# Carrying scale factors across partitions by DMA transposes of 16-bit powers of two, in a fused attention and Fourier kernel on one core

## The chip, the core and the metric

The kernel runs on one core of a Trainium2 chip. The core has a matrix engine (TensorE, PE in the profile, with its weight loads as PEld), VectorE (DVE), ScalarE (ACT), GpSimd (POOL) and a queue that issues most of the transfers (SyncE, SP). Each engine works through its own list of instructions in order and waits at an instruction until what it depends on is done; so an instruction that waits holds up all that stand behind it in the same list. The engines share an on-chip memory of 128 partitions; products land in banks of a second memory, PSUM, that ACT and DVE read out. The metric is the device time of one execution, in microseconds (us); lower is better.

## What is computed

Two independent layers are computed on inputs of 2048 x 1024, and their outputs are put side by side. Cut to what matters:

```python
def _A_ref(x, wqkv, wo):            # H = 32 heads of Dh = 32, window W = 256
    qkv = (x @ wqkv).reshape(B, S, 3, H, Dh).transpose(2, 0, 3, 1, 4)
    q, k, v = qkv[0], qkv[1], qkv[2]
    scores = einsum("bhqd,bhkd->bhqk", q, k) * Dh ** -0.5
    mask = (i - j >= 0) & (i - j < W)
    p = softmax(where(mask, scores, -1e9), axis=-1)
    o = einsum("bhqk,bhkd->bhqd", p, v)
    return o.transpose(0, 2, 1, 3).reshape(B, S, D) @ wo

def _B_ref(x, seq_re, seq_im, hid_re, hid_im):
    a = einsum("bsd,ed->bse", x, hid_re)
    b = einsum("bsd,ed->bse", x, hid_im)
    return einsum("ts,bse->bte", seq_re, a) - einsum("ts,bse->bte", seq_im, b)

out = concatenate([A_ref(...), B_ref(...)], axis=-1)
```

All inputs and the output are float32.

## The kernel before

**Number format.** A float32 matrix is multiplied as two float16 parts. Each operand is divided by a power of two, its scale, so that it fits float16; `split` (L124) writes the high part on ACT and the remainder, the low part, on DVE. A product is then three passes over float16 parts (`PASSES`, L48), 12 or 24 matmuls into one PSUM bank.

**Scales.** A scale needs the largest value (or mean size) of a whole block, over all 128 partitions. `top` (L142) or `mean` (L150) leaves one number for each partition; `spread` (L157) joins the pieces to one column, `top_...` in the traces. `scale_of` (L166) brings it across the partitions: PE transposes the column, broadcast to 128x128, against an identity matrix (`ident`) into a PSUM tile `pt_...`; DVE takes the maximum of each row, keeps the exponent bits (an AND with 0x7F800000), clamps and shifts it, and takes the reciprocal. There are four such scales for weights and two for inputs in the head of the kernel, two more for inputs behind it, and then two for `wv`, one for `wo`, two for the hidden matrices (`wd`), eight each for the blocks of B's input (`xp`) and for `wk`, four for `wq`, and 32 for blocks of the sequence matrices (`u`).

**Stages.** First the products for q, k and v (`order`, L390), 24 matmuls each, with the preparation of B's operands beside them by a table of due steps (`at`, L397): step n of that table runs just ahead of product n. Then 48 units (`units`, L742): 16 of kind x, for B's hidden transform, and 32 of kind c, for its sequence transform, each made by `seven` (L1027) as seven products instead of eight, in positions 0 to 6 over three banks in the order a, b, a, c, a, b, a. Position 4 ends in bank a and DVE adds it to the output (`add`, L1034, instruction line L1035), after which position 6 adds further products to the same bank. The last stage is the output projection (`po`), in the same form.

**A unit's preparation.** While unit n-2 runs, `u_top` (L754) sums two loaded blocks on ACT (`junk`), `spread` joins the two, and in the last turn `u_scale` (L765) makes the scale; while unit n-1 runs, `u_step` (L793) splits into `un_a`, `un_b`, `un_c` and a part kept in `reg`.

**Attention** runs as a generator (`attention`, L210), advanced by `tick` (L363) a step at a time between the matmuls of the products and units. One block of 128 queries of two heads makes scores `s` on PE, a masked maximum `mx` on DVE, exponentials on ACT, a float16 pair `hl`, and a DMA transpose of `hl` to `t` (L272). Six blocks later `v_step` multiplies by v. After four blocks `o_step` (L322) divides, transposes the result to `ot` by DMA (L335) and lists a store of `ot` to memory (`store_o`), which is issued at L354 in the next fourth block.

**What sets the order.** The program is written in one sequence and a scheduler places instructions on each engine by its own estimate of durations; `issue_after` pins some to follow another. `fixed` pins PE's matmuls to program order, `behind`, `behind_act`, `marks` and `line` (the last of the pinned loads and of the transposes to `t`) pin others. All transfers named here, transposes included, are issued by SP's one list.

Of the kernel before, what the change touches and what calls it, by code (L numbers as in the profile page):

```python
# [9 lines left out]
F32 = mybir.dt.float32  # L10
F32R = mybir.dt.float32r
F16 = mybir.dt.float16
BF16 = mybir.dt.bfloat16
U8 = mybir.dt.uint8
U32 = mybir.dt.uint32
AF = mybir.ActivationFunctionType
ALU = mybir.AluOpType
# [2 lines left out]
P = 128  # L20
S = 2048
D = 1024
H = 32
# [30 lines left out]
def fused_kernel(ctx: ExitStack, tc: tile.TileContext, xa, wqk, wv, wo, xb, wd, cs, out):  # L54
# [23 lines left out]
    tsum = reg1[:, :7 * 8 * CH].rearrange("p (s h k c) -> p s h k c", s=7, h=2, k=4)  # L78
    spare = reg1[:, 7 * 8 * CH:]

    ident = const.tile([P, P], F32, name="ident")
    make_identity(nc, ident)


    upper = const.tile([P, P], F32, name="upper")
# [8 lines left out]
    pshift = const.tile([P, 1], F32, name="pshift")  # L94
    nc.gpsimd.memset(pshift, PSHIFT)

    nbank, units_on = [0], []

    def bank(name):
        nbank[0] += 1  # L100
        return ps_m.tile([P, CH], F32, tag=f"m{nbank[0] % 3}", name=name)
# [31 lines left out]
        return const.tile([P, 2], F32, name=f"sc_{name}")  # L133

    tops, head = {}, [True]


    behind = []
# [18 lines left out]
    def spread(key, n):  # L157
        t = tops.pop(key)
        if n > 1:
            t1 = small.tile([P, 1], F32, tag="top0", name=f"top1_{key}")  # L160
            vec(nc.vector.tensor_reduce, t1, t, axis=AX.X, op=ALU.max)
        else:
            t1 = t
        tops[key] = t1

    def scale_of(key, v, s, down=2.0 ** -14):  # L166

        if head[0]:
            pt = ps_s.tile([P, CH], F32, tag="s", name=f"pt_{key}")[:, :P]
            with tc.issue_after(fixed[0].ins) if fixed else nullcontext():  # L170
                fixed[:] = [nc.tensor.transpose(pt, tops.pop(key).to_broadcast([P, P]), ident)]
        else:
            pt = (ps_v.tile([P, CH], F32, tag="pv", name=f"pt_{key}") if units_on else bank(f"pt_{key}"))[:, :P]
            nc.tensor.transpose(pt, tops.pop(key).to_broadcast([P, P]), ident)
        vec(nc.vector.tensor_reduce, v, pt, axis=AX.X, op=ALU.max)
        vec(nc.vector.tensor_scalar, v.bitcast(U32), v.bitcast(U32), 0x7F800000, None, op0=ALU.bitwise_and)
        vec(nc.vector.tensor_scalar, v, v, 2.0 ** -100, down, op0=ALU.max, op1=ALU.mult)
        vec(nc.vector.reciprocal, s, v)
# [31 lines left out]
    def attention():  # L210
# [127 lines left out]
        for b in range(nblk + LAG):  # L338
            for j in range(2):
                yield (blocks[b][0], blocks[b][2]) if b < nblk else None  # L340
                if b < nblk and j == 0:
                    s_step(b, 0)
                    s_step(b, 1)
                if j == 1 and b % 2 == 0 and b >= LAG:
                    v_step(b - LAG)
                    g, hp, sc, i = blocks[b - LAG + 1]
                    if i == QB - 1:
                        o_step(g, hp, sc)
                if j == 1 and b % 2 == ZAT and 3 <= b < nblk + 4:
                    for m in (b - 3 - (ZAT == 0), b - 2 - (ZAT == 0)):  # L350
                        if 0 <= m < nblk:
                            z_step(m)
                if j == 1 and store_o and (b >= nblk or blocks[b][3] == 3):
                    nc.sync.dma_start(*store_o.pop(0))  # L354
                if j == 1 and b < nblk and blocks[b][3] == 1 and b + 3 < nblk:
                    g, hp, sc, _ = blocks[b + 3]
                    if (g, sc) in ready:
                        do_load(g, hp, sc)
# [38 lines left out]
    def at(n, f, *args):  # L397
        tasks.setdefault(n, []).append((f, args))
# [151 lines left out]
    for (kd, g), n in use.items():  # L550
        if kd in "qk" and n >= 4:
            at(n - 6, w_load, kd, g)
            at(n - 4, w_top, kd, g)
            at(n - 3, w_finish, kd, g)
    for g in range(NG):
        at(max(use["q", g], use["k", g], 11), scores_scale, g)

# [3 lines left out]
        at(n, x_split, 0, (i,), behind_act)  # L561
    at(7, strict.__setitem__, 0, False)
    at(7, head.__setitem__, 0, False)
    at(4, x_top, 2, (0, 1))
    at(5, x_top, 2, (2, 3))
    at(7, x_finish, 2)
# [4 lines left out]
    at(11, x_known)  # L571
    at(11, wv_load, 0)
    at(14, wv_top, 0)
    at(15, wv_scale, 0)
    for i, n in enumerate((15, 16, 16, 17)):
        at(n, wv_split, 0, (i,))
    at(15, wv_load, 1)
    at(18, wv_top, 1)
    at(19, wv_scale, 1)
    for i, n in enumerate((19, 20, 21, 21)):  # L580
        at(n, wv_split, 1, (i,))
    at(20, wv_known)
    def scan(key, ns):
# [292 lines left out]
    at(len(order) - 3, x_left, 0, "c")  # L876


    with tc.tile_pool(name="pa", bufs=2) as pa:
        def qk_out(kd, g, c, ps, f):  # L880
            y = pa.tile([P, 2, CH], F16, tag="yq", name=f"y{kd}{g}_{c}")
            behind_act[:] = [nc.scalar.activation(y[:, 0], ps, AF.Copy, scale=f)]
            behind[:] = [vec(nc.vector.scalar_tensor_tensor, y[:, 1], ps, f, y[:, 0],
                             op0=ALU.mult, op1=ALU.subtract)]
            a = "qk".index(kd)
            nc.sync.dma_start(qk[g, c, a:a + 2, :, :, a].rearrange("j d h t -> (d h) j t"), y)
            nc.sync.dma_start(qk[g, c, 2 - 2 * a, :, :, a].rearrange("d h t -> (d h) t"), y[:, 0])

        def d_out(g):
            qk_out("q", g, 0, direct.pop(g), f0[:, g:g + 1])  # L890

        w_top("q", 0)
        x_top(0, (0, 1, 2, 3))
        d_mm(0, range(0, 4))
        w_scale("q", 0)
        d_mm(0, range(4, 8))
        w_top("q", 1)
        d_mm(1, range(0, 1))
        x_scale(0)
        d_known(0)  # L900
        d_mm(1, range(1, 3))
        w_scale("q", 1)
        d_known(1)
        d_out(0)
        w_split("q", 0)
        w_top("q", 2)
        d_mm(1, range(3, 8))
        x_top(1, (0, 1))
        d_out(1)
        d_mm(2, range(0, 2))  # L910
        w_scale("q", 2)
        d_known(2)
        x_top(1, (2, 3))
        d_mm(2, range(2, 8))
        w_top("q", 3)
        d_mm(3, range(0, 2))
        x_scale(1)
        x_split(1, (0, 1))
        d_out(2)
        d_mm(3, range(2, 4))  # L920
        w_scale("q", 3)
        d_known(3)
        x_split(1, (2,))
        d_mm(3, range(4, 8))
        x_split(1, (3,))
        w_split("q", 1)
        d_out(3)

        for n, (kd, g, c) in enumerate(order):
            if n < 4:  # L930
                continue
            if n == 22:
                first_cm.__exit__(None, None, None)
                att_cm = tc.tile_pool(name="att", bufs=2, side="right")
                cell["att"] = att_cm.__enter__()
                agen[0] = attention()
                upcoming[0] = next(agen[0])
            for f, args in tasks.pop(n, ()):
                f(*args)
            rate[0] = 2 * early * EARLY.get(n, 0.85) / 24  # L940
            ps = bank(f"p{kd}{g}_{c}")
            if kd == "v":
                t = c
                product(ps, lambda h, d: xin[:, t // 4, h, d, t % 4 * P:t % 4 * P + P],
                        lambda h, d: reg2[:, g, h, d])
                y = pa.tile([P, H // 2, VW], F16, tag="yv", name=f"yv{g}_{t}")
                nc.gpsimd.memset(y[:, :, DH:DH + 1], 1.0)
                nc.gpsimd.memset(y[:, :, 2 * DH + 1:], 0.0)
                f = vf[:, g, t // 4:t // 4 + 1]
                pv = ps.rearrange("p (h d) -> p h d", d=DH)  # L950
                behind_act[:] = [nc.scalar.activation(y[:, :, :DH], pv, AF.Copy, scale=f)]
                behind[:] = [nc.vector.scalar_tensor_tensor(y[:, :, DH + 1:2 * DH + 1], pv, f, y[:, :, :DH],
                                                            op0=ALU.mult, op1=ALU.subtract)]
                nc.sync.dma_start(vs[t, :, g * (H // 2) * VW:(g + 1) * (H // 2) * VW],
                                  y.rearrange("p h w -> p (h w)"))
            else:
                u = wun[kd, g]
                product(ps, lambda h, d: u[:, h, d], lambda h, d: xin[:, c, h, d])
                qk_out(kd, g, c, ps, DOWN if kd == "q" else kf[:, c:c + 1])
            if kd == "v" and g == 0 and c % 4 == 3:  # L960
                ready.add((0, c // 4))
            if kd == "v" and g == 1 and c == NT - 1:
                pass
            if kd == "k" and g > 0:
                ready.add((g, c))
# [116 lines left out]
            hook(pos)  # L1082


    units_on.append(True)
    perm, turns = [(nbank[0] + 1 + k) % 3 for k in range(3)], [0]
    with tc.tile_pool(name="pb", bufs=1) as pb:
        ybufs = [pb.tile([P, 2, CH], F32, name=f"y{k}") for k in range(3)]
        ybufs.append(spare[:, 16 * P:].bitcast(F32).rearrange("p (e c) -> p e c", e=2))
        ny = [0]  # L1090
# [154 lines left out]
```

## Time and profile before

| | |
|---|---|
| Time, median of three runs | 1716.21 us (1709.82 to 1716.93) |
| Profiled execution, its own time | 1715.44 us |
| Its span, first to last instruction | 1713.7 us |
| Granted TensorE clock | 1.00 |
| Chain of work that ended last | PE 84%, DMA 5%, DVE 4%, ACT 4% |
| Transfers | 348.63 MB, mean 203 GB/s |
| Transposes by DMA: `t` and `ot` | 256 and 64 |

The page of the profile gives the busy time of each engine, then the span in 40 slices in which a digit is the busy share in tenths. A group of instructions reads "line, engine, operation, output<-inputs, shapes, count | busy us, mean ns of one | idle time of the engine before them, and who ended it". In the list of waits a row reads "engine, its line, who it waited for: us in total, times, longest". In a timeline a row is "start, duration, engine, line, operation, output<-inputs, shapes, count", with idle time before it in brackets. Of an issued transfer "to landing" is the time until its data are there. The chain's 84% for PE, with nothing else above 5%, says that the end is set by what PE does or waits for.

### The profile page before, as it was taken

Reading aid. Unit: us, or ns where it says so; the run is one execution under the profiler, and the core shown is the slowest. Engines: PE = TensorE matmul, PEld = TensorE weight load, DVE = VectorE, ACT = ScalarE, POOL = GpSimd, SP = SyncE. Lnnn points to the kernel's source line nnn. Section 1 sums busy time; section 2 is a strip of 40 time slices with the busy share of each in tenths; the row PEclk is TensorE's granted clock in tenths of the full one; section 3 lists DMA queues with packets and bytes.
Section 4 is the critical chain, followed back from the end, with each engine's and each line's share of the span. In section 5 each row is a group of like instructions: output and inputs, shape, how many; then the busy total and the mean of one; then the engine's idle time right before and its main releaser. Section 6 shows DMA issues by size and latency. Waiting matters only on the chain.

```text
span 1713.7 us, 30874 instructions
## 1 busy us (share of the span) xinstructions
PE 1694.8 (99%) x10999; PEld 852.4 (50%) x10999; DVE 1302.1 (76%) x2225; ACT 1170.1 (68%) x2035; POOL 575.5 (34%) x874
## 2 busy tenths in 40 slices
PE   9999999999999999999999999999999989999999
PEld 4444555555555544555554555545545545444444
DVE  6847788887987788887688886698876698688442
ACT  4566666676877787887687886688876678563322
POOL 0001222344434441444423565434565424411000
PEclk9999999999999999999999999999999999999999
DMA  9747999999998994887998999987999986875431
GB/s 349 245 137 242 252 291 289 271 262 299 243 245 198 215 226 121 206 196 182 229 244 241 196 182 181 223 196 127 197 169 185 203 203 127 166 193 118 117 98 74
DMA packets 469899, 348.63 MB, mean 203 GB/s; under 512 B 376944, under 2 KB 409968, under 8 KB 468848
## 3 DMA queue, kind: packets, MB, share of 16 engines
q1 hardware_dynamic: 462064, 321.48, 74.7%
q0 software_dynamic: 7680, 25.17, 9.2%
q8 instruction: 86, 1.41, 0.4%
q14 instruction: 69, 0.57, 0.1%
HBM read 166.99 MB, written 106.17 MB: 159 GB/s over the span
## 4 chain that ended last, share of the span: by engine, by line
PE 84%; DMA 5%; DVE 4%; ACT 4%; issue 2%; POOL 1%; SPq 0%; ACTq 0%; DVEq 0%; POOLq 0%
PE p_a L114 23%; PE pv L114 14%; PE p_b L114 11%; PE pk L114 9%; PE pq L114 9%; PE p_c L114 6%; PE po_a L114 5%; PE s L114 3%; PE po_b L114 2%; DMA raw_u<-in_cs_dram 2%; DMA t<-hl 1%; PE far L114 1%; PE po_c L114 1%; ACT reg L833 1%; DVE raw_u L791 1%
## 5 line engine op out<-in xcount | busy, mean ns | idle before, releaser
L266 ACT ACTIVATE s<-s,bias,escs 128x256 f32<-128x256 f32 (+1 forms) x512 | 270.1, 528 | 11.7
L284 POOL TENSOR_SCALAR_AFFINE_SELECT z<-t 128x512 f16<-128x512 f16 x224 | 186.4, 840 | 180.4 <-PE pv L114 137.4
L270 DVE TENSOR_TENSOR hl<-s,hl 128x512 f16<-128x512 f32 (+1 forms) x256 | 169.9, 664 | 61.6 <-ACT hl L269 59.5
L259 ACT ACTIVATE bias<-mx,pshift,escs 128x2 f32<-128x2 f32 x256 | 98.2, 384 | 169.3 <-DVE mx L256 168.8
L114 PEld LDWEIGHTS <-reg 128*128 128x128 f16 x1344 | 129.1, 98 | 141.5
L286 POOL TENSOR_SCALAR_AFFINE_SELECT t<-t 128x512 f16<-128x512 f16 x224 | 183.9, 830 | 11.4
L114 PE MATMUL p_a<-reg,un_c 128*128 128x512 f16 x768 | 181.2, 379 | 1.8 <-ACT y L1033 1.3
L114 PE MATMUL pk<-reg,wu_k 128*128 128x512 f16 x768 | 174.4, 379 | 0.0
L256 DVE TENSOR_REDUCE mx<-s 128x2 f32<-128x512 f32 (+1 forms) x256 | 170.7, 667 | 3.4
L114 PE MATMUL pv<-reg,reg 128*128 128x512 f16 x768 | 172.7, 379 | 0.0
L114 PEld LDWEIGHTS <-un_c 128*128 128x128 f16 x1152 | 110.0, 97 | 124.0 <-issue 4.9
L114 PEld LDWEIGHTS <-un_b 128*128 128x128 f16 x1152 | 110.1, 97 | 123.9 <-issue 7.8
L263 POOL TENSOR_SCALAR mark<-bias 128x1 f32<-128x1 f32 x128 | 52.3, 409 | 355.2 <-ACT bias L259 355.0
L114 PEld LDWEIGHTS <-un_a 128*128 128x128 f16 x1152 | 109.8, 97 | 116.2
L269 ACT ACTIVATE hl<-s 128x512 f16<-128x512 f32 (+1 forms) x256 | 148.8, 581 | 13.6 <-DMA t<-hl 8.3
L114 PE MATMUL pq<-reg,wu_q 128*128 128x512 f16 x672 | 151.3, 379 | 0.8 <-DVE reg L121 0.5
L114 PE MATMUL p_a<-reg,un_b 128*128 128x512 f16 x576 | 136.4, 379 | 4.7 <-DVE y L1035 3.0
L114 PE MATMUL p_b<-reg,un_b 128*128 128x512 f16 x576 | 136.3, 379 | 1.2 <-ACT y L1033 1.0
L114 PE MATMUL p_a<-reg,un_a 128*128 128x512 f16 x576 | 136.6, 379 | 0.0
L114 PE MATMUL p_c<-reg,un_a 128*128 128x512 f16 x576 | 136.5, 379 | 0.0
L254 DVE COPY_PREDICATED s<-upper,far 128x256 f32<-128x256 uint32 x224 | 94.2, 420 | 46.0 <-PE s L114 45.0
L114 PEld LDWEIGHTS <-qk 96*128 96x128 f16 x1056 | 87.9, 97 | 64.1 <-DMA qk<-qk 1.9
(208 smaller groups left out, 3154.1 us busy)
## 6 DMA issues: line engine op xcount, KB each, us to landing
raw_u<-in_cs_dram SPq DMA_DIRECT2D x64, 512.0 KB, 4.9
qk<-qk SPq DMA_DIRECT2D x64, 384.0 KB, 5.1
out_dram<-y POOLq DMA_DIRECT2D x72, 256.0 KB, 6.3
raw_wd<-in_wd_dram SPq DMA_DIRECT2D x24, 512.0 KB, 5.3
vs<-yv SPq DMA_DIRECT2D x32, 264.0 KB, 4.2
vt<-vs SPq DMA_DIRECT2D x64, 132.0 KB, 4.2
raw_wo<-in_wo_dram SPq DMA_DIRECT2D x16, 512.0 KB, 9.2
qk<-yq SPq DMA_DIRECT2D x32, 256.0 KB, 3.1
```

The costliest lines, as they stand in the source:

```text
L114: fixed[:] = [nc.tensor.matmul(*args, **kwargs)]
L254: nc.vector.copy_predicated(s[:, :, P:], upper2, d["far"] if nb == 3 else never2)
L256: nc.vector.tensor_reduce(mx, sv, axis=AX.X, op=ALU.max, negate=True)
L259: nc.scalar.activation(bias, mx, AF.Identity, bias=pshift, scale=es)
L263: marks[:] = [nc.gpsimd.tensor_scalar(mark, bias[:, 0:1], 1.0, None, op0=ALU.mult)]
L266: nc.scalar.activation(sv[:, h], sv[:, h], AF.Exp, bias=bias[:, h:h + 1], scale=es)
L269: nc.scalar.activation(hi, sv, AF.Copy)
L270: behind[:] = [nc.vector.tensor_tensor(lo, sv, hi, op=ALU.subtract)]
L284: nc.gpsimd.affine_select(out=z, in_=pk, compare_op=ALU.is_gt, fill=0.0, base=0, pattern=[[0, 4], [-1, P]], channel_multiplier=1)
L286: nc.gpsimd.affine_select(out=pk, in_=pk, compare_op=ALU.is_ge, fill=0.0, base=0, pattern=[[0, 4], [1, P]], channel_multiplier=-1)
L791: nc.vector.tensor_tensor(o, a, b, op=op)
L833: nc.scalar.activation(hi, src, AF.Copy)
```

## The change

Scales past the head no longer use PE. `spread` writes a 128x128 tile `pb` on DVE: the upper 16 bits of each partition's float32 number, ANDed with 0x7F80 and repeated along the row. These 16 bits are a power of two in the format bfloat16. SP issues a DMA transpose of `pb` to `pc`, and `scale_of` takes the maximum of each row of `pc`, then clamps, shifts and takes the reciprocal as before; the AND on the result is gone. The path is switched on at step 11 of the table, so the two scales of inputs that are made behind the head keep the transpose on PE.

The other edits: the store of `ot` is pinned to follow the last transpose or load in `line`; `ident` moves into a spare region that is free in the head; the output tiles of q, k and v share three buffers where there were two for q and k and two for v; scales and splits of the later `wq` and `wk` and of `wv` come one step later in the table.

```diff
         tops[key] = t1
+        if crossing[0]:
+            pb = crossing[0].tile([P, P], F16, tag="pb", name=f"pb_{key}")
+            nc.vector.tensor_scalar(pb.bitcast(U16), t1.bitcast(U16)[:, 1:2].to_broadcast([P, P]), 0x7F80, None,
+                                    op0=ALU.bitwise_and)
+            pc = crossing[0].tile([P, 1, P], F16, tag="pc", name=f"pc_{key}")
+            nc.sync.dma_start_transpose(pc, pb)
+            crossed[key] = pc.rearrange("p a t -> p (a t)").bitcast(BF16)
...
+        if key in crossed:
+            nc.vector.tensor_reduce(v, crossed.pop(key), axis=AX.X, op=ALU.max)
+            nc.vector.tensor_scalar(v, v, 2.0 ** -100, down, op0=ALU.max, op1=ALU.mult)
+            nc.vector.reciprocal(s, v)
+            return
...
-            pt = (ps_v.tile([P, CH], F32, tag="pv", name=f"pt_{key}") if units_on else bank(f"pt_{key}"))[:, :P]
+            pt = bank(f"pt_{key}")[:, :P]
...
-                    nc.sync.dma_start(*store_o.pop(0))
+                    with tc.issue_after(line[0].ins):
+                        nc.sync.dma_start(*store_o.pop(0))
...
-            at(n - 3, w_finish, kd, g)
+            at(n - 3 if n < 16 else n - 2, w_finish, kd, g)
...
+    at(11, lambda: crossing.__setitem__(0, pa))
...
-    at(15, wv_scale, 0)
-    for i, n in enumerate((15, 16, 16, 17)):
+    at(16, wv_scale, 0)
+    for i, n in enumerate((16, 17, 17, 18)):
...
-    ident = const.tile([P, P], F32, name="ident")
+    ident = spare[:, :2 * P].bitcast(F32)
...
-    with tc.tile_pool(name="pa", bufs=2) as pa:
+    with tc.tile_pool(name="pa", bufs=3) as pa:
...
-            y = pa.tile([P, 2, CH], F16, tag="yq", name=f"y{kd}{g}_{c}")
+            y = pa.tile([P, 2, CH], F16, tag="y", name=f"y{kd}{g}_{c}")
...
-                y = pa.tile([P, H // 2, VW], F16, tag="yv", name=f"yv{g}_{t}")
+                y = pa.tile([P, H // 2, VW], F16, tag="y", name=f"yv{g}_{t}")
...
     with tc.tile_pool(name="pb", bufs=1) as pb:
+        crossing[0] = pb
```

How this moves instructions is seen best in the unit stage. First DVE's list in unit 5, of before, from the joined column `top_u` of unit 7 to the addition after position 4 (`y<-p_5_a`) and the one after position 5 (`y<-p_5_b`); `un_c` and `un_b` are splits for unit 6, `s`, `mx`, `hl` and `o` are attention:

```order
L121 TENSOR_REDUCE top_u_8232<-top_u_8153 128x1
L254 COPY_PREDICATED s_8242<-upper,far 128x2x128
L256 TENSOR_REDUCE mx_8248<-s_8242 128x2
L270 TENSOR_TENSOR hl_8194<-s_8182,hl_8194 128x512
L121 SCALAR_TENSOR_TENSOR un_c<-raw_u_1_7756,sc_u_8072,un_c 128x1024
L1035 SCALAR_TENSOR_TENSOR y_6763<-p_5_a,fu_7878,y_6763 128x512
L254 COPY_PREDICATED s_8290<-upper,far 128x2x128
L121 SCALAR_TENSOR_TENSOR un_b<-raw_u_0_7834,sc_u_8072,un_b 128x1024
```

The same stretch in the changed kernel; `sc_u<-pc_u` is the reduction over the transposed tile:

```order
L123 TENSOR_REDUCE top_u_8259<-top_u_8180 128x1
L170 TENSOR_SCALAR pb_u_8261<-top_u_8259 128x128
L269 COPY_PREDICATED s_8273<-upper,far 128x2x128
L271 TENSOR_REDUCE mx_8279<-s_8273 128x2
L179 TENSOR_REDUCE sc_u_8425<-pc_u_8263 128x1
L180 TENSOR_SCALAR sc_u_8425<-sc_u_8425 128x1
L285 TENSOR_TENSOR hl_8221<-s_8209,hl_8221 128x512
L181 RECIPROCAL sc_u_8425<-sc_u_8425 128x1
L788 TENSOR_SCALAR fu_8429<-fa,sc_u_8425 128x1
L123 SCALAR_TENSOR_TENSOR un_c<-raw_u_1_7781,sc_u_8102,un_c 128x1024
L1052 SCALAR_TENSOR_TENSOR y_6787<-p_5_a,fu_7904,y_6787 128x512
```

The whole scale has moved ahead of `un_c` and of the addition after position 4 (L1035 of before is L1052 now). Before, the reduction `sc_u<-pt_u` stood 16 rows behind `top_u`, past both additions.

Second, SP's list at the same unit, of before, from a transpose to `ot` to the store of that `ot`:

```order
L335 DMA_TRANSPOSE ot_1_3_8120<-ohl_1_3_8117 128x4x128
L272 DMA_TRANSPOSE t_8052<-hl_8049 128x8x128
L354 DMA ots<-ot_1_3_8120 128x512
L272 DMA_TRANSPOSE t_8147<-hl_8144 128x8x128
L272 DMA_TRANSPOSE t_8197<-hl_8194 128x8x128
```

and of the changed kernel:

```order
L350 DMA_TRANSPOSE ot_1_3_8147<-ohl_1_3_8144 128x4x128
L287 DMA_TRANSPOSE t_8082<-hl_8079 128x8x128
L287 DMA_TRANSPOSE t_8174<-hl_8171 128x8x128
L173 DMA_TRANSPOSE pc_u_8263<-pb_u_8261 128x1x128
L287 DMA_TRANSPOSE t_8224<-hl_8221 128x8x128
L769 DMA raw_u_0_8390<-in_cs_dram 128x1024
L769 DMA raw_u_1_8523<-in_cs_dram 128x1024
L287 DMA_TRANSPOSE t_8290<-hl_8287 128x8x128
L370 DMA ots<-ot_1_3_8147 128x512
```

The store stood one transpose behind its `ot` and now stands four transposes to `t`, two loads and the new transpose to `pc` behind it.

More of the change, by code (lines that the diff above doesn't have):

```diff
@@ L14 @@
 U8 = mybir.dt.uint8
+U16 = mybir.dt.uint16
 U32 = mybir.dt.uint32
@@ L95, in fused_kernel @@
     nc.gpsimd.memset(pshift, PSHIFT)
-    nbank, units_on = [0], []
+    nbank = [0]
     def bank(name):
@@ L135, in fused_kernel @@
     tops, head = {}, [True]
+    crossing, crossed = [None], {}
     behind = []
@@ L578, in fused_kernel @@
     at(18, wv_top, 1)
-    at(19, wv_scale, 1)
-    for i, n in enumerate((19, 20, 21, 21)):
+    at(20, wv_scale, 1)
+    for i, n in enumerate((20, 21, 21, 22)):
         at(n, wv_split, 1, (i,))
@@ L1082, in seven @@
             hook(pos)
-    units_on.append(True)
     perm, turns = [(nbank[0] + 1 + k) % 3 for k in range(3)], [0]
     with tc.tile_pool(name="pb", bufs=1) as pb:
+        crossing[0] = pb
         ybufs = [pb.tile([P, 2, CH], F32, name=f"y{k}") for k in range(3)]
```

## The prediction

> **What bounds the kernel now.** I read the page first: engine totals, then the 40 slices.
>
> ```profile
> span 1713.7 us, 30874 instructions
> ...
> PE 1694.8 (99%) x10999; PEld 852.4 (50%) x10999; DVE 1302.1 (76%) x2225; ACT 1170.1 (68%) x2035; POOL 575.5 (34%) x874
> ...
> PE   9999999999999999999999999999999989999999
> ...
> DVE  6847788887987788887688886698876698688442
> ```
>
> TensorE (PE) is full in every slice but one, so only two things can shorten the kernel: fewer PE instructions, or less of the 1713.7 - 1694.8 = 18.9 us in which PE stands still. VectorE (DVE) is second, near eight tenths through the middle. Next the waits of PE alone, then the windows over two stages.
>
> ```profile
> PE p_a L114 <- DVE y L1035: 4.4, 6, 1.7
> PE p_a L114 <- ACT p_c L1067: 2.3, 5, 1.1
> ...
> PE s L114 <- DMA qk<-qk: 1.4, 1, 1.4
> ...
> PE pt_u L174 <- DVE o L318: 0.6, 1, 0.6
> ```
>
> ```profile
> 300.00:400.00 100.00, 100.00 (x697) 51.61 (x696) 86.80 (x156) 69.31 (x124) 39.84 (x77) 1.00 1.02 274
> ...
> 920.00:1050.00 130.00, 127.83 (x925) 66.59 (x924) 109.58 (x197) 101.51 (x187) 74.62 (x99) 1.00 0.97 177
> ```
>
> Columns are the stretch, its length, busy time of PE, PEld, DVE, ACT, POOL, then clock, DMA share and GB/s. Where PE waits at all, it mostly waits for one DVE instruction: the addition at L1035 that empties bank a after position 4 of a seven-product unit, so that position 6 may add onto the bank. In the unit stage (920 to 1050 us) DVE works 84% of the time, and that addition is where its lateness becomes PE's.
>
> **The part removed: 57 transposes.** Seven groups at L174 go; the two of pt_x stay, as do those of the head (L171).
>
> ```profile
> L174 PE MATMUL pt_u<-ident,top_u 128*128 128x128 f32 x32 | 8.8, 274 | 0.6 <-DVE o L318 0.6
> ...
> L174 PE MATMUL pt_wk<-ident,top_wk 128*128 128x128 f32 x8 | 2.2, 273 | 0.0
> L174 PE MATMUL pt_xp<-ident,top_xp 128*128 128x128 f32 x8 | 2.2, 273 | 0.0
> L174 PE MATMUL pt_wq<-ident,top_wq 128*128 128x128 f32 x4 | 1.1, 280 | 0.0
> ...
> L174 PE MATMUL pt_wv<-ident,top_wv 128*128 128x128 f32 x2 | 0.5, 272 | 0.0
> L174 PE MATMUL pt_wd<-ident,top_wd 128*128 128x128 f32 x2 | 0.5, 272 | 0.0
> L174 PE MATMUL pt_wo<-ident,top_wo 128*128 128x128 f32 x1 | 0.3, 302 | 0.0
> ```
>
> 32+8+8+4+2+2+1 = 57. Their 274 ns is a duration in a pipeline, not what PE loses. The timeline of PE around one shows the loss:
>
> ```profile
> 630.63 1.03 PE L114 MATMUL p_a<-reg,un_a 128*128 128x512 f16 x4
> 631.49 0.27 PE L174 MATMUL pt_u<-ident,top_u 128*128 128x128 f32 x1
> 631.60 1.89 PE L114 MATMUL p_a<-reg,un_a 128*128 128x512 f16 x8
> ```
>
> Starts are 0.11 us apart, while four products before it took 0.86 us. So 57 x 0.11 = 6.3 us leave PE; without further effects 1715.4 becomes 1709.1.
>
> **The part added: a wait inside DVE's queue.** A scale now goes DVE (pb), SP queue, DMA transpose, DVE again (the reduction over pc). DVE runs in order. By the order of the changed kernel the reduction stands none to six rows behind pb, and in 29 of the 32 units it stands ahead of the L1035 addition after position 4; before, it stood behind both additions and waited only for PE. What is queued behind the waiting reduction is thus the split un_c, that addition, and the attention's DVE work; PE's position 6 waits for the addition. The unit whose order is shown above, in the trace of before:
>
> ```profile
> 682.24 0.14 DVE L121 TENSOR_REDUCE top_u<-top_u 128x1 f32<-128x2 f32 x1
> ...
> 685.10 1.28 DVE L121 SCALAR_TENSOR_TENSOR un_c<-raw_u,sc_u,un_c 128x1024 f16<-128x1024 f32 x1 [0.92 <-ACT un_c L127]
> 686.30 0.74 DVE L1035 SCALAR_TENSOR_TENSOR y<-p_a,fu,y 128x512 f32<-128x512 f32 x1
> ```
>
> ```profile
> 688.23 1.89 PE L114 MATMUL p_a<-reg,un_b 128*128 128x512 f16 x8
> ```
>
> The addition starts 4.06 us after top_u and ends at 687.04; PE takes up position 6 at 688.23: 1.19 us to spare. I took the same three times in all 32 units; the first and the last:
>
> ```profile
> 622.32 0.14 DVE L121 TENSOR_REDUCE top_u<-top_u 128x1 f32<-128x2 f32 x1
> ...
> 625.11 0.74 DVE L1035 SCALAR_TENSOR_TENSOR y<-p_a,fx,y 128x512 f32<-128x512 f32 x1
> ```
>
> ```profile
> 627.81 1.89 PE L114 MATMUL p_a<-wx,un_c 128*128 128x512 f16 x8
> ```
>
> ```profile
> 1520.81 0.14 DVE L121 TENSOR_REDUCE top_u<-top_u 128x1 f32<-128x2 f32 x1
> ...
> 1523.87 0.74 DVE L1035 SCALAR_TENSOR_TENSOR y<-p_a,fu,y 128x512 f32<-128x512 f32 x1
> ```
>
> ```profile
> 1525.68 2.75 PE L114 MATMUL p_a<-reg,un_b 128*128 128x512 f16 x12
> ```
>
> Means over the 32: the addition starts 4.1 us after top_u, ends at 4.8, PE comes at 5.7. The spare time is 0.9 us, and below 0.7 in 17 units.
>
> Now the new chain, with L the time from the end of pb to the landing of pc. No row shows a 128x128 transpose, nor pb. The nearest DVE rows:
>
> ```profile
> L121 DVE TENSOR_REDUCE sc_u<-pt_u 128x1 f32<-128x128 f32 x32 | 9.0, 282 | 8.2 <-PE pt_u L174 8.2
> ...
> L121 DVE TENSOR_SCALAR sc_u<-sc_u 128x1 uint32<-128x1 uint32 x32 | 4.8, 149 | 0.6
> ```
>
> Both pb and the new reduction lie between 0.15 and 0.28 us; I take 0.15 and 0.25, which leaves DVE's work about as it was (one 0.15 and one 0.28 go). For L, the transposes of four tiles (ot) and of eight (t), each row taken from the answer on its tile or line:
>
> ```profile
> L335 SPq DMA_TRANSPOSE ot<-ohl x64: 1188/1213/2481, 194.3 to 1486.7; - x64
> ...
> DMA to landing us min/median/max: 1.7/3.8/10.4
> ```
>
> ```profile
> DMA to landing us min/median/max: 2.3/4.8/14.8
> ```
>
> SP spends 1.2 us issuing even the smallest. Landing counts from the start of the issue. From eight tiles to four the median falls by 1.0 us, 0.25 a tile; one tile would be 3.8 - 3 x 0.25 = 3.05 us. Half an issue of another transpose ahead of it in SP's queue adds 0.6: L = 3.6 us, an estimate. Its ends are 1.7, the least that four tiles took, and 4.8, the median of eight; the 3.6 is nearer the four-tile median, which carries the same fixed part.
>
> In the 29 units the mean work between top_u and pb is 0.2 us and from the reduction to the addition 1.3 us (durations as in the grouped rows, by the new order). The addition then ends 0.1 + 0.2 + 0.15 + L + 0.25 + 1.3 + 0.74 = 2.7 + L after top_u. Against PE's 5.7 that is free up to L = 3.0, and at 3.6 costs 0.6 us a unit, 29 x 0.6 = 17 us. Unit by unit, where spare time cannot be shared, I get 4 us at L = 2.5, 11 at 3.0, 21 at 3.5, 32 at 4.0 and 58 at 5.0, so about 23. I take 20 us.
>
> **The other edits.** The 25 other crossings make DVE wait too, between 80 and 525 us; the pt_wk rows are the first and last of them:
>
> ```profile
> L174 PE MATMUL pt_wk<-ident,top_wk x8: 272/273/275, 81.7 to 523.9; 128*128 128x128 f32 x8
> ```
>  There PE refills one of three banks only two products later, at least 2 x 24 x 0.215 = 10 us; that covers a wait of 3 us: 0, at worst 5 if DVE, 87% busy at 300 to 400 us, lacks the room. Splits of weights one step later still have two steps of 5 us: 0. The shared y buffers and ident in the spare region touch no wait of PE's: 0. The later store of ot frees SP:
>
> ```profile
> SPq L354 <- DMA ot<-ohl: 134.9, 58, 9.1
> ```
>
> SP's queue stood 134.9 us behind that store, 2.3 each; 57 new issues of 1.2 us take 68 back. PE waits for none of the transfers behind it except 1.4 us once, so I put 0 here, and 2 us of gain as the end. Sum: 1715.4 (the profiled execution; span 1713.7 and 1.7 around it; the median of three runs is 0.8 higher) - 6.3 + 20 = 1729 us.
>
> [...]
>
> **Rivals.**
> - *The wait is hidden.* L is 3.0 or less, or DVE reaches top_u earlier because it has nothing else to do: 0 to 11 us of stall, 1709 to 1720 us. For it: the best four-tile landing, 1.7 us, and the 64 KB loads in the row below. Against: the DMA engines are 97% busy in the window of 920 to 1050 us, and 3.8 is the median.
>
> ```profile
> raw_o<-ots SPq DMA_DIRECT2D x128, 64.0 KB, 2.4
> ```
>
>  [...]
> - *The stalls of before go too.* The later store lets transposes land sooner, DVE is less behind, and the 4.4 us on L1035 shrink: 1715.4 - 6.3 - 4.4 - 2 = 1703, range 1701 to 1707.
> - *SP's queue is the price.* The pc transpose sits behind loads that wait for buffers, L is 4.5 to 5: 45 to 58 us, 1754 to 1767.
>
> **How the numbers follow.** Forecast, 1720 to 1741: 0.45. Hidden: 0.33. Stalls go too: 0.10. SP's queue: 0.12. Half a per cent of 1716.2, 8.6 us, is about what a measurement of this kernel tells from no change: faster is below 1707.6, slower above 1724.8. Slower: 0.12 and 0.38 of the forecast's share, 0.50. Faster: 0.10 and 0.06 for the low edge of the hidden case, 0.16. The rest, 0.34, is the same. The range of 8 in 10 runs from 1704, inside the third case, to 1750, which leaves SP's queue out.
>
> **What would show it.** PE: 57 fewer transposes and busy time about 6 us down. DVE: a wait of sc_u on the DMA of pc, 1 to 3 us each, some 60 us in all. PE: p_a waiting for y at the L1035 addition some 25 times instead of 6, for 15 to 30 us. SP: the wait of the store on ot nearly gone. I am wrong if pc lands within 3 us of pb, if the addition is late without PE noticing, or if PE waits elsewhere, for s or pv.

## The result, and the profile after

| | before | changed |
|---|---|---|
| Time, median | 1714.89 us (six runs, 1709.82 to 1718.91) | 1786.51 us (six runs, 1782.17 to 1791.03) |
| Ratio, 95% interval | | 1.042 (1.0394 to 1.0446) |
| Profiled execution: its own time, span | 1715.44, 1713.7 us | 1782.17, 1780.1 us |
| Granted TensorE clock | 1.00 | 0.991 |

The changed kernel is 4.2% slower. The sign was forecast and the size was not: 1729 us was predicted, and the range ended at 1750. The page of the changed kernel answers to the lines shown before: span, busy time of each engine, slices of PE and DVE, and the chain that ended last.

```profile
span 1780.1 us, 30857 instructions
...
PE 1709.4 (96%) x10942; PEld 848.5 (48%) x10942; DVE 1308.0 (73%) x2225; ACT 1167.6 (66%) x2035; POOL 566.2 (32%) x874
...
PE   9999999999999999999998999999999999999999
...
DVE  6757768887887778887687776688687698577542
...
PE 57%; DVE 17%; DMA 9%; ACT 8%; issue 6%; POOL 2%; SPq 1%; DVEq 0%; POOLq 0%; ACTq 0%
```

Two numbers of the PE row tell where to look. PE stands still for 1780.1 - 1709.4 = 70.7 us, against 18.9 before: 51.8 us more. And it is busy for 14.6 us longer although 57 of its instructions are gone (10999 to 10942). Together that is 66.4 us, the whole difference of the spans. The row of slices hardly shows either, since a slice is 44 us long and "9" covers everything above 90%. The chain does: PE's share fell from 84% to 57%, and DVE and the DMA engines took its place.

Next, the waits of PE in the changed kernel (who waited, for whom, us in total, times, longest), and the three largest waits of DVE on the new transposes. `far` is the attention's PSUM tile for the scores of the oldest keys of the window; `p_c` is bank c, which ACT fills with a copy of bank a after position 0.

```profile
PE p_a L116 <- DVE y L1052: 32.4, 19, 4.4
PE far L116 <- DVE s L269: 13.5, 14, 2.3
PE p_a L116 <- ACT p_c L1084: 9.3, 7, 3.9
PE p_a L116 <- DVE sc_u L180: 3.9, 2, 3.5
PE far L116 <- DVE vwd L180: 1.4, 1, 1.4
```

```profile
DVE sc_u L179 <- DMA pc_u<-pb_u: 72.4, 29, 5.9
...
DVE scw L179 <- DMA pc_wk<-pb_wk: 18.4, 8, 5.5
...
DVE vxp L179 <- DMA pc_xp<-pb_xp: 14.3, 6, 5.6
```

The addition after position 4 (L1052, which was L1035) is the largest, as forecast: 32.4 us against 4.4. None of the four rows below it was in the prediction's sum; of them only the copy `p_c` stood in the waits that it showed, with 2.3 us. Two of the rows name an instruction that ended right beside the one that PE needed. At 1076.37 us (`sc_u`, 3.5 us) PE started 0.06 us after the addition's end, and so it did in the other `sc_u` wait on bank a; at 411.01 us (`vwd`) it started 0.05 us after the end of DVE's masking (L269), for which `far` waits. Counted there, PE waited 36.3 us for the addition and 14.9 for the masking.

Two windows place the loss by stage (length, busy time of PE, granted clock, DMA share, GB/s); in the trace of before the same two stages, from 80 us to the first unit product at 566 and from there to the output projection at 1564.5, took 486.0 and 998.5 us.

```profile
80.00:582.60 502.60, 486.59 (x3188) 0.99 0.91 242
582.60:1631.10 1048.50, 999.37 (x6784) 0.99 0.85 181
```

So the qkv stage lost 16.6 us and the units 50.0.

One unit shows the mechanism at full length. The timeline of DVE and then of PE in the changed kernel (start, duration, instruction, and in brackets the idle time before it and who ended it):

```profile
1041.15 0.23 DVE L170 TENSOR_SCALAR pb_u<-top_u 128x128 uint16<-128x128 uint16 x1
1047.31 0.29 DVE L179 TENSOR_REDUCE sc_u<-pc_u 128x1 f32<-128x128 bf16 x1 [5.93 <-DMA pc_u<-pb_u]
1047.52 1.27 DVE L123 SCALAR_TENSOR_TENSOR un_c<-raw_u,sc_u,un_c 128x1024 f16<-128x1024 f32 x1
...
1049.10 0.74 DVE L1052 SCALAR_TENSOR_TENSOR y<-p_a,fu,y 128x512 f32<-128x512 f32 x1
```

```profile
1049.90 1.04 PE L116 MATMUL p_a<-reg,un_b 128*128 128x512 f16 x4 [4.41 <-DVE y L1052]
...
1051.38 3.28 PE L116 MATMUL p_a<-reg,un_b 128*128 128x512 f16 x8
```

DVE finishes pb and has nothing it may do: the next instruction on its list is the reduction over pc, which can start only 5.93 us later. For 1.2 us of that the transpose stood in SP's list behind a transpose to `t`; it landed 4.7 us after the start of its issue at 1042.55 us. The split un_c and the addition, which need nothing from that DMA, stand behind it. PE waits 4.41 us for the addition. Then the second price appears: the eight products that follow take 3.28 us, where eight take 1.89 elsewhere. A window tells why (columns as above):

```profile
1051.00:1052.00 1.00, 1.00 (x6) 0.50 0.98 344
1052.00:1053.00 1.00, 1.00 (x4) 0.50 2.83 224
1053.00:1054.00 1.00, 1.00 (x4) 0.50 0.05 5
```

PE was granted half its clock for 3.41 us, from 1050.77 us on. This trace has eight such stretches, 30.7 us together; PE was busy in 29.7 us of them, so half of that, 14.9 us, went into doing the same work more slowly. Three theories were put to the test. **Theory 1**: the wait in DVE's list stops PE, and the pauses cost clock on top. **Theory 2**: 57 more transposes on SP's list and the DMA engines slow everything. **Theory 3**: the other edits of the change cost the time.

### The profile page after: what moved, and what is told of

Its sections match the earlier page's. It is cut to its first block, busy times and chain, and to the rows that moved or that the text cites. A ratio compares the mean times of both kernels' runs of the same rounds, so it can differ in the third digit from the quotient of the medians.

```text
span 1780.1 us, 30857 instructions
## 1 busy us (share of the span) xinstructions
PE 1709.4 (96%) x10942; PEld 848.5 (48%) x10942; DVE 1308.0 (73%) x2225; ACT 1167.6 (66%) x2035; POOL 566.2 (32%) x874
## 4 chain that ended last, share of the span: by engine, by line
PE 57%; DVE 17%; DMA 9%; ACT 8%; issue 6%; POOL 2%; SPq 1%; DVEq 0%; POOLq 0%; ACTq 0%
PE p_a L116 17%; PE pv L116 8%; PE p_b L116 7%; PE pq L116 6%; DMA pc_u<-pb_u 5%; PE po_a L116 5%; PE p_c L116 4%; PE pk L116 4%; PE po_b L116 2%; DVE mx L271 2%; PE s L116 2%; ACT s L281 2%; DVE raw_u L808 1%; DVE hl L285 1%; DVE reg L851 1%
## 5 line engine op out<-in xcount | busy, mean ns | idle before, releaser
L116 PE MATMUL p_a<-reg,un_b 128*128 128x512 f16 x576 | 146.3, 399 | 34.9 <-DVE y L1052 27.1
L269 DVE COPY_PREDICATED s<-upper,far 128x256 f32<-128x256 uint32 x224 | 94.4, 421 | 37.8 <-PE s L116 37.1
```

Of the source, the lines that this page charges most:

```text
L116: fixed[:] = [nc.tensor.matmul(*args, **kwargs)]
L269: nc.vector.copy_predicated(s[:, :, P:], upper2, d["far"] if nb == 3 else never2)
```

## The experiments

**Late reductions.** All stays as in the changed kernel, but the reduction over pc is pinned behind the last addition or remainder (`hl`, `y`) that was written ahead of it. By the order of the program it stood one to seven rows behind pb and, in 29 units, ahead of both additions; now it stands behind both in all 32.

```diff
         if key in crossed:
-            nc.vector.tensor_reduce(v, crossed.pop(key), axis=AX.X, op=ALU.max)
+            with tc.issue_after(behind[0].ins) if behind else nullcontext():
+                nc.vector.tensor_reduce(v, crossed.pop(key), axis=AX.X, op=ALU.max)
```

> Changed kernel, with the reduction over pc pinned behind the last addition or remainder that was written ahead of it, so that in all 32 units it stands behind both additions on VectorE's list; DMA transposes and all other edits stay. Theory 1 (VectorE's list stands at the reduction and TensorE then waits for the addition and for the scores, and loses clock): 1704 to 1716 us, TensorE's waits for y under 8 us in all, none for far above 1 us, clock 1.00. Theory 2 (57 more transposes load SP's list and the DMA engines): stays at 1775 to 1790. Theory 3 (the other edits): stays at 1775 to 1790.

Measured: 1722.35 us (1710.69 to 1726.55), 1.0033 of before (1.0008 to 1.0059). With every transpose still there, some 64 us of the 72 are gone, and Theories 2 and 3 fall as main causes. DVE's waits on all tiles pc shrink from 122 us (72.4 + 18.4 + 14.3 in the rows above, and 17.1 in four smaller ones) to 20:

```profile
DVE sc_u L180 <- DMA pc_u<-pb_u: 14.6, 2, 13.8
...
DVE vwd L180 <- DMA pc_wd<-pb_wd: 4.3, 1, 4.3
...
DVE vxp L180 <- DMA pc_xp<-pb_xp: 0.8, 1, 0.8
```

The time missed Theory 1's 1704 to 1716. The waits for the addition came out as expected, 2.8 us; but the clock was 0.996 instead of 1.00, and `far` waited 2.9 us where at most 1 was expected. PE's waits show what cost the time: one long pause.

```profile
PE p_a L116 <- ACT p_c L1085: 12.4, 1, 12.4
PE s L116 <- DMA qk<-qk: 2.9, 1, 2.9
PE far L116 <- DVE vwd L181: 2.9, 1, 2.9
PE p_a L116 <- DVE y L1053: 2.8, 5, 1.0
```

Its cause is read from SP's timeline. The transpose for unit 46 was issued right behind eight loads of `raw_wo`, 512 KB each by their shape (128 x 1024 float32), and landed 15.7 us after its issue, the longest of all:

```profile
1496.23 3.95 SPq L224 DMA_DIRECT2D raw_wo<-in_wo_dram  x8
1500.28 1.15 SPq L173 DMA_TRANSPOSE pc_u<-pb_u  x1
```

**The last two units by TensorE.** To see whether that one transpose explains the miss, the kernel with late reductions was run again with the scales of units 46 and 47 by TensorE.

```diff
                     att_cm.__exit__(None, None, None)
+                    crossing[0], id2[0] = None, upper
+                    make_identity(nc, upper)
...
-            pt = bank(f"pt_{key}")[:, :P]
-            nc.tensor.transpose(pt, tops.pop(key).to_broadcast([P, P]), ident)
+            last = id2[0] is not None
+            pt = (ps_v.tile([P, CH], F32, tag="pv", name=f"pt_{key}") if last else bank(f"pt_{key}"))[:, :P]
+            nc.tensor.transpose(pt, tops.pop(key).to_broadcast([P, P]), id2[0] if last else ident)
```

> The kernel with late reductions once more, but the scales of the last two units go by TensorE again (against an identity tile written over the mask, which nobody needs by then). Theory 1, with the loss of the first run put down to the one transpose that landed 15.7 us after its issue, behind eight loads of raw_wo: the pause of 12.4 us and the half clock behind it go, 1703 to 1709 us, clock 1.00. If the loss came from the transposes in general (Theory 2): 1718 to 1724 as in the first run.

Measured: 1711.77 us (1705.77 to 1713.40), 0.9979 (0.9955 to 1.0004). The pause of 12.4 us is gone, and with it 10.6 us (9 by the two ratios, whose intervals do not overlap), so it was the cause of most of the miss; yet the time stays some 3 us above the range that was given. One pause in the qkv stage is left, of the same kind: `far` waits for DVE, which waited for the transpose of `wd`, and again the products behind it are slow (eight in 3.62 us).

```profile
402.25 0.27 PE L116 MATMUL far<-qk 96*128 96x128 f16 x1 [3.53 <-DVE vwd L181]
...
402.84 3.62 PE L116 MATMUL pk<-reg,wu_k 128*128 128x512 f16 x8
```

**The other edits alone.** Every scale goes by TensorE as before, `ident` stays where it was, and what is left of the change is the pinned store of `ot`, the shared y buffers and the later steps.

```diff
-    at(11, lambda: crossing.__setitem__(0, pa))
...
-        crossing[0] = pb
...
-    ident = spare[:, :2 * P].bitcast(F32)
+    ident = const.tile([P, P], F32, name="ident")
```

> All other edits of the change (store of ot pinned, three shared y buffers, scales and splits one step later), but every scale by TensorE as before, and ident where it was. Theory 1: 1710 to 1718 us, as before. Theory 2: the same, since no transposes are added. Theory 3: 1760 or more.

Measured: 1707.65 us (1705.61 to 1709.93), 0.9969 (0.9957 to 0.9982). Theory 3 has the wrong sign: the other edits gain, and the time lies below the 1710 to 1718 of the other two theories too. The same kernel, measured once more beside a kernel shown below:

> The kernel with the other edits alone, once more on the same chip, for the comparison with the kernel above: 1706 to 1709 us, 0.995 to 0.999 of the kernel before.

Measured: 1710.14 us, 0.9962 (0.9945 to 0.9979). The gain is small but both intervals lie below 1, and of all kernels run this one has the lowest ratio.

**The pinned store alone**, to see which of these edits gains: the kernel before with one edit.

```diff
-                    nc.sync.dma_start(*store_o.pop(0))
+                    with tc.issue_after(line[0].ins):
+                        nc.sync.dma_start(*store_o.pop(0))
```

> The kernel before, with the store of ot pinned behind the last transpose or load, and nothing else. If the gain of the kernel with the other edits alone (1707.65 against 1713.72 us) comes from the freed list of SP: 1705 to 1710. If it comes from the later scales and splits or the shared y buffers: 1712 to 1716.

Measured: 1710.22 us (1707.34 to 1711.67), 0.9974 (0.9955 to 0.9993): the gain is this edit's, as far as the intervals can tell the two kernels apart. SP's wait for `ot` at the store, 134.9 us before, is 6.9 us; PE's waits for the addition fall from 4.4 us to this:

```profile
PE p_a L114 <- DVE y L1036: 0.8, 3, 0.3
```

**Transposes that nobody reads.** The kernel with the other edits alone, and besides it 55 of the 57 pb tiles and transposes are made and left unread (those of the last two units are left out). For want of room they have one buffer each, not three.

```diff
         if crossing[0]:
-            pb = crossing[0].tile([P, P], F16, tag="pb", name=f"pb_{key}")
+            pb = crossing[0].tile([P, P], F16, tag="pb", bufs=1, name=f"pb_{key}")
...
-            crossed[key] = pc.rearrange("p a t -> p (a t)").bitcast(BF16)
```

> As the kernel with the other edits alone (scales by TensorE), and 55 of the 57 pb tiles and DMA transposes to pc are made too, with nobody reading pc. Theory 1: within 6 us of the kernel with the other edits alone, about 1712 to 1722 us. Theory 2: 1770 or more, with TensorE waiting for qk, vt or t. Theory 3: equal to the kernel with the other edits alone.

Measured: 1716.91 us (1714.16 to 1719.29), 1.0008 (0.9990 to 1.0026), 9.3 us above the kernel with the other edits alone, where Theory 1 allowed 6. But the place is telling. From the first unit product to the output projection this kernel takes 1566.1 - 574.0 = 992.1 us, the one without transposes 1556.7 - 566.2 = 990.5: thirty transposes cost 1.6 us. The other 7.8 lie in the qkv stage, where the single buffer made DVE wait again, pb now standing behind the transpose of the one before it:

```profile
DVE pb_wq L170 <- DMA pc_wd<-pb_wd: 5.2, 1, 5.2
DVE pb_xp L170 <- DMA pc_wk<-pb_wk: 3.2, 1, 3.2
DVE pb_wo L170 <- DMA pc_xp<-pb_xp: 1.4, 1, 1.4
```

So this run says little about traffic in the qkv stage, and in the units it leaves Theory 2 next to nothing.

**Only the units.** The changed kernel, with the 25 scales of the qkv stage by TensorE against a second identity tile.

```diff
-    at(11, lambda: crossing.__setitem__(0, pa))
+    def second_ident():
+        id2[0] = pa.tile([P, P], F32, tag="id", bufs=1, name="ident2")
+        make_identity(nc, id2[0])
+    at(9, second_ident)
```

> Changed kernel with the DMA path in the 32 units alone; the 25 scales of the qkv stage go by TensorE against a second identity tile. Theory 1, if the two stages add: the first p_a at about 566 us instead of 582.6, the unit stage still 48 to 52 us longer than before, 1768 to 1772 us. Theory 2, if the cost goes by the number of transposes: 32/57 of 72 us, about 1755. Theory 3: 1780 to 1790.

Measured: 1766.06 us (1764.88 to 1771.09), 1.0311 (1.0274 to 1.0348), some 2 us below Theory 1's range and 11 above Theory 2's figure. The first unit product comes at 565.8 us, as without any transposes (566.2 in the kernel with the other edits alone), and the unit stage is as long as in the changed kernel (565.8 to 1615.3, 1049.5 us). The two stages add, and in the units the waits of PE are those of the changed kernel:

```profile
PE p_a L116 <- DVE y L1055: 34.2, 19, 7.1
PE p_a L116 <- ACT p_c L1087: 10.9, 7, 5.2
```

**The DMA path where it does least harm**: thirty units, with late reductions; everything else by TensorE. It combines the diffs above, and asks whether a crossing that nobody waits for is worth its transpose.

> The DMA path where it does least harm: in 30 of the 32 units, with late reductions; the 25 scales of the qkv stage and the last two units by TensorE; all other edits of the change. Theory 1, if a crossing that nobody waits for is free: 30 x 0.11 = 3.3 us under the kernel with the other edits alone, about 1703 to 1706. If late scales or 30 more transposes still cost something in the units: 1708 to 1713, no better than the kernel with the other edits alone.

Measured: 1713.14 us (1710.32 to 1716.85), 0.9986 (0.9965 to 1.0007), beside 0.9962 for the kernel with the other edits alone. The 3.3 us that Theory 1 gave a free crossing do not show; the intervals overlap, so a small loss isn't shown either. Taking transposes off PE gains nothing here that can be measured.

**Pauses by themselves.** Is it the pause that lowers the clock, or something else in the changed kernel? In the kernel before, 14 pauses are put into the output projection, where PE works without a stop (from 1565 us on the trace of before lists no wait of PE's) and no attention, unit or transpose runs beside it. GpSimd starts from a column of an output tile, works on a scratch tile for a set time, and a small matmul reads that tile.

```diff
+            if pos in (2, 4):
+                wake()          # mm(dps[:, :16], junk16[:, 3], junk16[:, 3, :16])
...
                 copy(y2[:, 1], ps)
+                sleep_from(y2[:, 1])
```

> The kernel before, with 14 pauses of TensorE put into the output projection, where nothing else stops it: a small matmul waits for a chain of GpSimd operations sized for pauses of 1.0 to 5.0 us (2.0, 4.0, 2.5, 1.5, 3.5, 3.0, 2.0, 5.0, 2.5, 1.0, 3.0, 4.5, 2.25, 2.75 in this order); the small matmul adds a product that nobody reads. If a pause itself lowers the granted clock: half clock for 3 to 7 us after each pause above about 4 us, after none below 1.9, and after some in between, so that busy time rises by 2 to 3.5 us a case. If the half clock of the changed kernel came from something else (the transposes, the load of the unit stage): the clock stays 1.00 behind all 14.

Measured: 1749.93 us in one run. The pauses came out shorter than planned, 26.6 us in all and 3.4 at the longest, so the case above 4 us went untested. Three of the 14 were followed by half clock:

```profile
1575.39 0.18 PE L114 MATMUL dps<-junk 128*128 128x16 f16 x1 [2.52 <-POOL junk L1040]
1575.43 2.75 PE L114 MATMUL po_c<-reg,raw_o 128*128 128x512 f16 x12
...
1583.32 0.18 PE L114 MATMUL dps<-junk 128*128 128x16 f16 x1 [2.55 <-POOL junk L1040]
1583.36 4.14 PE L114 MATMUL po_b<-wx,raw_o 128*128 128x512 f16 x12
...
1621.48 0.18 PE L114 MATMUL dps<-junk 128*128 128x16 f16 x1 [2.75 <-POOL junk L1040]
1621.52 4.44 PE L114 MATMUL po_c<-reg,raw_o 128*128 128x512 f16 x12
```

Twelve products take 2.75 us at full clock, and 4.44 behind the pause of 2.75 us: 1.7 us lost, where 2 to 3.5 were expected for a case. The third case was the pause of 3.36 us. The pauses of 2.52 and 3.13 us were followed by none, nor was any below 2.2. So a pause is enough, without attention, units or transposes beside it; but its length does not decide alone. The last section shows what sorts these cases.

## Why the prediction was wrong

**The mechanism was right.** DVE waits on the transpose in the units 29 times, SP's wait at the store fell from 134.9 to 9.2 us, PE has 57 instructions fewer, and the largest new wait is the addition's. Putting the reduction late took some nine tenths of the loss away. But one of the signs of being wrong that the prediction named came as well: PE waited elsewhere, though not for `s` or `pv`.

**Step (the wait inside DVE's queue): mis-sized.** The prediction put L at 3.6 us and took 20 us for the addition, in some 25 waits. PE waited 36.3 us for it, 31.9 more than before, in 21 waits. The measured L, from the end of pb to the start of the reduction, has a median of 3.6 us over the 32 units, but a mean of 4.1 and a longest of 11. The prediction's own sum, done unit by unit, gives 23 us with 3.6 for all 29 units and 30 with each unit's measured L (an estimate from the same rows of before): the spread is worth some 7 us, because a stall grows with the long cases and isn't paid back by the short ones. Another 3 us went when 23 was taken as 20, and the last 6 stay unexplained. That the prediction's table has 32 us at L = 4.0, next to the row's 32.4, is chance: the row leaves out the two waits named `sc_u`, and L was not 4.0 in every unit.

**What made L long.** Not SP's list, as the rival *SP's queue is the price* had it: from the end of pb to the start of the issue 0.6 us passed in the mean, from there to the landing 3.4. In the median it was 0.1 and 2.6.

**Step (the 25 other crossings, put at 0): wrong.** It looked at the three banks of the products, and between 80 and 582 us PE indeed waited for none of these. PE has a second thing to wait for in that stage: `far`, one PSUM tile in two halves, which DVE's masking (L269) frees. That instruction stood behind the reduction too. PE waited 14.7 us for it between 80 and 582 us (the row of `vwd` included) and not once before the change, and two of the eight stretches at half clock lie there: 16.6 us for the stage.

**Missing from the sum: others that DVE serves.** ACT's copy to the third bank (p_c) came late too, 9.3 us against 2.3. In the longest of these waits, 3.87 us, ACT had stood 3.53 us at the split un_a until DVE had made the scale, and the copy stood behind that split in ACT's list. The prediction followed one consumer of DVE's list and left out the rest of them.

**Missing from the sum: the clock.** The stretches at half clock cost 14.9 us. The pauses experiment shows that a pause can bring this on: half clock followed three of its 14. It was no rival in the prediction, and it is three quarters of the 20 us that were forecast for the addition.

**Step (the later store, 0 to -2): too small.** It gains about 4 us alone (0.9974 of 1715), and the rival *the stalls go too* was right about its mechanism. The change as measured hides it under the loss.

**The removed transposes, -6.3.** Their number is confirmed. Their worth isn't: the kernel with 30 fewer and late reductions was no faster than the one with all of them.

In terms of the two profiled executions: addition +31.9, masking +14.3 (14.9 against 0.6) and p_c +7.0 make +53.2 of idle time, and small waits that shrank bring it to the measured +51.8. Transposes -6.3 and clock +14.9 make +8.6 of busy time, where +14.6 were measured. No run shows where the other 6.0 are. An estimate: the timeline counts a tail of 0.17 us as busy ahead of a pause (the four products that start 0.86 us before the next instruction are written as 1.03 us), and PE has 52 pauses above 0.15 us instead of 22, which makes 5 us. The predicted sum was -6.3 + 20.

**The transfer itself.** The tile pc_u, 32 KB, landed 2.2 us after the start of its issue at the least, 2.6 in the median and 9.6 at the most. The median is near the 2.4 us that plain transfers of 64 KB (`raw_o`) took in the same trace; the long cases, which made the stalls, are another matter. Counted from the end of the issue, the median of the 32 is 1.3 us; SP's issue of 1.1 us or more and the wait ahead of it come on top, and L as a whole was never below 2.2 us. Of the kernels that carry scales across by DMA none had a ratio below 0.9979; the one with the other edits alone had 0.9969 and 0.9962.

What stays open: whether the 2 to 3 us between the kernel with late reductions (last two by TensorE), 0.9979, and the kernel with the other edits alone, 0.9969 and 0.9962, are real, since the intervals overlap; and if they are, how much is traffic and how much is the one pause that is left.

## What to carry to other kernels

A step that is moved from a fast engine to a DMA must not be judged by the engine time it frees but by where its consumer stands in an in-order list: put the consumer behind everything that doesn't need it (here that alone took the kernel from 1.042 of before to 1.0033). For the price of such a wait, list every consumer of the waiting engine, not the one that showed up before, and use the spread of the latency (2.3 to 11 us here) rather than its median (3.6). And count what a pause of the matrix engine costs after it is over, 14.9 us here.

## What the runs showed of the hardware

PE's clock halved behind a pause of 1.98 us and not behind one of 3.50 us. In the changed kernel, with products or scores behind the pause:

```profile
387.92 0.22 PE L116 MATMUL far<-qk 96*128 96x128 f16 x1 [1.98 <-DVE s L269]
```

```profile
975.16 4.44 PE L116 MATMUL p_a<-reg,un_b 128*128 128x512 f16 x12 [2.27 <-DVE y L1052]
```

```profile
1076.37 2.75 PE L116 MATMUL p_a<-reg,un_b 128*128 128x512 f16 x12 [3.50 <-DVE sc_u L180]
```

The first two were followed by a clock of 0.50 for 3.41 us, the third, after 3.50 us, was not. Counted over all traces of this study, for pauses that the timeline puts down to one instruction: none that stood alone and was shorter than 1.9 us was followed by half clock, 3 of 13 from 1.9 to 2.2 were, 13 of 21 from there to 4.0, and 7 of 7 above 4.3.

The record of the granted clock, from which the clock of the windows is made, shows what sorts them. In the changed kernel the eight stretches of 0.50 begin at 388.59, 470.51, 975.68, 1023.47, 1050.77, 1269.23, 1337.49 and 1528.64 us. Seven of them last 3.413 us and the last one 6.827; and from start to start it is 24, 148, 14, 8, 64, 20 and 56 times 3.413 us. So in this trace the changes of the clock lie on a grid of 3.413 us. Now each pause of 1.9 us or more can be cut at that grid, in every trace that has such a stretch. All of the 20 pauses with 2.1 us or more inside one cell were followed by half clock from the start of the next cell on; none of the 13 with less than 1.9 us in any cell was; of the eight between, 1.91 to 2.03 us, three were (the changed kernel's share of these is six, five and four pauses, two of the four followed). The pause of 3.50 us above had at most 1.80 us in one cell and was free; the one of 1.98 us lay in one cell and was not. In the pauses experiment the pause of 2.52 us had 1.45 us in one cell and was free, and the one of 2.55 us had 2.18 and was not.

All this is a reading of traces, not an experiment: no run set the start of a pause against the grid.
